# Three loads of 64 KiB rows put ahead of a decode-attention kernel's first load

## The chip, the cores and the metric

The kernel runs on one core of one Trainium2 chip. The time is device time in microseconds, from the start of the program to its end. The kernel before was timed in two runs: median 1936.92 us (1936.79 to 1937.05). A profile is one execution taken by the hardware profiler; its span goes from the first to the last instruction.

## What is computed

Two independent blocks, A and B, of the same shape. Each takes one new token for 2 batch rows, makes its query, attends over a cache of 8192 positions with 32 heads of 192, and projects the result. Everything is bf16.

```python
# x: (2, 1, 640)   k_cache, v_cache: (2, 32, 8192, 192)   wq: (640, 6144)   wo: (6144, 640)
def _A_ref(x, k_cache, v_cache, wq, wo):
    B, Sq, D = x.shape
    Hq, Dh = 32, 192
    Hkv = k_cache.shape[1]
    rep = Hq // Hkv                                   # 1
    q = (lambda x, *d: x.transpose(*d))((x @ wq).reshape(B, Sq, Hq, Dh), 0, 2, 1, 3)
    k = jnp.repeat(k_cache, rep, axis=1)
    v = jnp.repeat(v_cache, rep, axis=1)
    scores = jnp.einsum("bhqd,bhkd->bhqk", q, k) * (Dh ** -0.5)
    p = _softmax(scores, axis=-1)
    o = jnp.einsum("bhqk,bhkd->bhqd", p, v)
    return (lambda x, *d: x.transpose(*d))(o, 0, 2, 1, 3).reshape(B, Sq, Hq * Dh) @ wo
# B is the same with its own inputs; the two results are concatenated on the last axis
```

The four caches hold 2 x 32 x 8192 x 192 elements each, 805 MB in all, and each of their bytes is needed once. The four weights are 31 MB together.

## The kernel before

**Units.** The work on the caches is cut into 64 units (`NU`): 2 blocks, 16 pairs of heads, 2 batch rows. A unit loads one K tile and one V tile. Each tile is 128 rows of 49152 B: the first 64 rows are the 8192 positions of one head, 128 to a row, the other 64 those of the next head. A tile is 6144 KB.

**The large tile.** `big` has 86016 bf16 elements (172032 B) in each of its 128 partitions. Three buffers of 24576 elements (`kv[0]` to `kv[2]`) lie at its start, and the tiles take them in turn: K of unit 0, K of unit 1, V of unit 0, K of unit 2, V of unit 1 and so on (`loads`, line 213). Behind them are two areas of 6144 elements for the products. Before the first units run, the two query weights lie in the same bytes: A's from element 24576 on, B's from 55296 on (`wq_off`, line 186). At the end, the output weights lie there too.

**A unit.** VectorE multiplies a K tile with the query, broadcast over the positions, in four chunks (`dve_mul`, L290). TensorE sums the products over the 192 elements by matmuls with the identity (`pe_sum`, L367), VectorE finishes the sum and takes the maximum, GpSimd spreads the maximum over the partitions, ACT takes the exponentials, and TensorE makes the weighted sum of V (`pe_pv`, L381).

**The start.** The query of all heads is made first. The x rows are spread over the partitions by TensorE and VectorE (`pe_x`, L350, and `dve_xbc`, L276), then 32 products with the query weights (`pe_q`, L359) are copied out by VectorE and ACT (L280, L285). Nothing of it can begin before the two x rows have landed.

**SyncE's queue.** All loads but one go through SyncE, one after the other, in the order in which the code writes them out. `ld_first`, 4 KB from ACT's queue, is the exception; nothing reads what it loads, and only the output waits for it. Each engine's work is a list (`_Stream`), whose `add` takes a function that issues an instruction and the events to wait for; the wait stands on that engine, and what is behind it in the list waits too. The order on SyncE is: a first piece of A's query weight (4096 B of each of the 128 rows, 512 KB), the rest of it (57344 B of each, 7168 KB), x of A and of B, B's query weight (61440 B rows, 7680 KB), and then the tiles. A tile's load waits until the tile that held its buffer three loads earlier has been used. The first piece of the weight is issued before the block of the engine programs begins (line 493), all others inside.

`dma` (line 247) makes a load and gives it an event of its own; such an event has come when all of the load has landed.

Of the kernel before, what the change touches and what calls it, by code (L numbers as in the profile page):

```python
# [117 lines left out]
def build_kernel(nc, blocks, out):  # L118
# [28 lines left out]
    with ExitStack() as es:  # L147
# [7 lines left out]
        big = sb("big", [128, NBUF * BUFE + 2 * PRODE], BF16)  # L155
# [39 lines left out]
        S_sp = _Stream("sp", sem("s_sp"), reg)  # L195
# [6 lines left out]
        def dsem(k, n=1):  # L202
            reg[k] = (sem("d_" + "_".join(str(i) for i in k)), 16 * n)
# [4 lines left out]
        for blk in range(NBLK):  # L208
            dsem(("wq", blk), len(wq_cut[blk]))
            dsem(("odone", blk))  # L210
        dsem(("first",))

        loads = [("k", 0)]
        for u in range(1, NU):
# [13 lines left out]
        for blk, rows, off, w in ((0, (WR,), woA, [("s", LASTU, NCH - 1)]), (1, (29,), wo0, [("pv", LASTU - 1)]),  # L228
                                  (1, (11, 5, 2, 1), wo1, [("pv", LASTU)])):
            r = 29 if off == wo1 else 0  # L230
            for n in rows:
                pieces.append((blk, r, r + n, off, w))
                off, r, w = off + n * D, r + n, []
# [9 lines left out]
        def back(name, u, c, n):  # L243
            i = u * NCH + c - n
            return (name, i // NCH, i % NCH) if i >= 0 else None

        def dma(out_ap, in_ap, k):
            s = reg[k][0]
            return lambda eng: eng.dma_start(out_ap, in_ap).then_inc(s, 16)  # L249

        def ld_x(blk):
            return dma(x4[B * blk:B * blk + B, :], blocks[blk]["x"][:, 0, :], ("x",))

        def ld_wq(blk, n):
            lo, hi = wq_cut[blk][n]
            src = blocks[blk]["wq"].rearrange("(j c) n -> j (c n)", c=DC)
            return dma(big[:, wq_off[blk] + lo:wq_off[blk] + hi], src[:, lo:hi], ("wq", blk))

        def ld_wo(n):
            blk, r0, r1, off, _ = pieces[n]  # L260
            src = blocks[blk]["wo"].rearrange("(p i) n -> p (i n)", i=WR)
            return dma(big[:, off:off + (r1 - r0) * D], src[:, r0 * D:r1 * D], ("wo", n))
# [177 lines left out]
        for u in range(NU):  # L440
            for c in range(NCH):
                w = [("k", u), ("pq", NP - 1), ("qa", NP - 1), ("qx", NP - 1), back("s", u, c, 2)]
# [32 lines left out]
        for n, p in enumerate(pieces):  # L475
            w = [("wo", n), ("ot", p[0])]
# [8 lines left out]
        def done(i):  # L485
            if i < 0:
                return None
            kind, u = loads[i]
            return ("m", u, NCH - 1) if kind == "k" else ("pv", u)

        ld_first = dma(first[:], blocks[0]["wq"].rearrange("(j c) n -> j (c n)", c=DC)[0:128:8, 0:128], ("first",))
        ld_first(nc.scalar)
        ld_wq(0, 0)(nc.sync)
        S_sp.add(ld_wq(0, 1))
        for blk in range(NBLK):
            S_sp.add(ld_x(blk))
# [1 line left out]
        for i, (kind, u) in enumerate(loads):  # L498
            w = [done(i - NBUF)]
            if i in (1, 2):  # L500
                w = [("pq", PPB * i - 1)]
# [8 lines left out]
        for n in range(1, HP + 1):  # L510
            S_pool.add((lambda n: (lambda eng: eng.memset(tri[0:n, n:n + 1], 1.0)))(n),
                       waits=[("tri0",)] if n == 1 else [], sig=("tri",) if n == HP else None)
# [5 lines left out]
        for n in range(128 // HP):  # L518
# [3 lines left out]
                  waits=[("id1",), ("place0",)], sig=("place",))  # L522
# [50 lines left out]
def bass_concat_heads__gqa_block_cached__mha_block_cached__decode_kernel(  # L573
    nc: bass.Bass,
    A_x: bass.AP,
    A_k_cache: bass.AP,
    A_v_cache: bass.AP,
    A_wq: bass.AP,
    A_wo: bass.AP,
    B_x: bass.AP,  # L580
    B_k_cache: bass.AP,
    B_v_cache: bass.AP,
    B_wq: bass.AP,
    B_wo: bass.AP,
    out: bass.AP,
):
    blocks = [
        dict(x=A_x, k=A_k_cache, v=A_v_cache, wq=A_wq, wo=A_wo),
        dict(x=B_x, k=B_k_cache, v=B_v_cache, wq=B_wq, wo=B_wo),
    ]  # L590
    build_kernel(nc, blocks, out)
# [28 lines left out]
```

## Time and profile before

| what | value |
|---|---|
| median of two runs | 1936.92 us |
| the profiled execution: span | 1935.4 us |
| TensorE busy | 1507.4 us (78%) |
| VectorE busy | 1123.0 us (58%) |
| ACT, GpSimd busy | 142.4 us (7%), 28.6 us (1%) |
| read from DRAM | 836.77 MB |
| DMA time of SyncE's queue (q1), share of 16 engines | 99.9% |

The median is 1.5 us above the span of the profiled execution; of that execution the page gives the span and no other time. An engine's busy time counts its instructions, without waiting; the share of q1 counts the time that packets took on the 16 DMA engines. In the lists of groups, a line such as "L290 DVE" names the line of the kernel, the engine, what is written and read, the number of instructions, their busy time, the mean of one, and the idle time ahead of them with what ended it. "us to landing" in the lists of DMAs goes from the issue by the engine to the arrival of the last byte.

### The profile page before, as it was taken

To read this page: it belongs to the slowest core of one execution; us is meant where nothing else is said; L and a number is where in the kernel's file an instruction comes from. 1 tells how busy PE (TensorE), PEld (TensorE's weight loads), DVE (VectorE), ACT (ScalarE), POOL (GpSimd) and SP (SyncE) were. 2 spreads that over 40 slices of the span, in tenths; PEclk is the share of its full clock that TensorE was granted. 3 is DMA by queue.
4 is the path that set the end of the run, shared out by engine and by line. 5 is a ranking of instruction groups with operands and counts; after the bars stand their busy time and mean duration, and the time that the engine had idled before them with its cause. 6 is when DMAs were issued, how large, how long until landed. Compare 5 with 4: busy or idle time off the path is not lost.

```text
span 1935.4 us, 19062 instructions
## 1 busy us (share of the span) xinstructions
PE 1507.4 (78%) x7729; PEld 732.1 (38%) x7729; DVE 1123.0 (58%) x907; ACT 142.4 (7%) x519; POOL 28.6 (1%) x113
## 2 busy tenths in 40 slices
PE   5777878878878878878878877877877877877878
PEld 2333433433433433434433433433433433433434
DVE  4765565565565565565565565565565565565560
ACT  3100000000000000000000000000000000000000
POOL 0000000000000000000000000000000000000000
PEclk9899999999999999999999999999999999999998
DMA  9999999999999999999999999999999999999999
GB/s 423 424 435 438 430 434 437 434 431 437 436 429 436 437 430 434 438 432 433 437 436 428 437 435 430 436 437 430 435 437 432 433 437 435 430 436 437 429 435 394
DMA packets 19786, 836.92 MB, mean 432 GB/s; under 512 B 2232, under 2 KB 2368, under 8 KB 2752
## 3 DMA queue, kind: packets, MB, share of 16 engines
q1 hardware_dynamic: 19744, 836.78, 99.9%
q8 instruction: 6, 0.10, 0.0%
q14 instruction: 4, 0.03, 0.0%
q10 hardware_dynamic: 32, 0.00, 0.0%
HBM read 836.77 MB, written 0.01 MB: 432 GB/s over the span
## 4 chain that ended last, share of the span: by engine, by line
DMA 49%; PE 29%; DVE 17%; issue 5%; DVEq 0%; SPq 0%; ACT 0%; ACTq 0%
DMA big<-in_B_k_cache_dram 25%; DMA big<-in_A_k_cache_dram 22%; PE ops L381 18%; DVE big L290 15%; PE scps L367 9%; DVE sc L294 2%; DMA big<-in_B_wo_dram 1%; PE scps L359 1%; DMA xw<-in_B_x_dram 1%; PE outps L359 0%; PE ops L373 0%; DVEq L290 0%; DVE qall L280 0%; PE scps L409 0%; SPq L249 0%
## 5 line engine op out<-in xcount | busy, mean ns | idle before, releaser
L290 DVE TENSOR_TENSOR big<-big,qall 128x6144 bf16<-128x6144 bf16 x256 | 852.8, 3352 | 522.0 <-DMA big<-in_B_k_cache_dram 275.3
L367 PE MATMUL scps<-big,ident 128*128 128x512 bf16 x3072 | 777.8, 411 | 395.3 <-DVE big L290 393.0
L381 PE MATMUL ops<-big,pb 128*34 128x384 bf16 x4096 | 676.8, 326 | 0.0
L367 PEld LDWEIGHTS scps<-big,ident 128*128 128x128 bf16 x3072 | 303.3, 104 | 863.1 <-DVE big L290 483.6
L381 PEld LDWEIGHTS ops<-big,pb 128*34 128x34 bf16 x4096 | 395.5, 98 | 258.7
L294 DVE TENSOR_REDUCE sc<-scps 128x32 f32<-128x512 f32 x256 | 176.0, 687 | 196.8 <-PE scps L367 196.8
L320 ACT ACTIVATE nb<-mg 64x1 f32<-64x1 f32 x128 | 25.7, 201 | 1707.1 <-POOL mg L271 1706.4
L329 ACT ACTIVATE pb<-sc,nb 64x128 bf16<-64x128 f32 x128 | 55.8, 436 | 7.8
L271 POOL PARTITION_ALL_REDUCE mg<-mp x64 | 25.9, 404 | 1857.9 <-DVE mp L300 1857.9
L300 DVE TENSOR_REDUCE mp<-sc 64x1 f32<-64x128 f32 x128 | 35.9, 280 | 8.3
L314 ACT ACTIVATE qall<-o_sum,rc 2x192 f32 (+1 forms) x64 | 29.0, 453 | 20.7 <-DVE o_sum L311 19.1
L311 DVE TENSOR_TENSOR o_sum<-ops,o_hi 2x192 f32<-2x192 f32 x64 | 22.1, 345 | 7.7
L359 PE MATMUL scps<-big,xw 128*128 x120 | 23.2, 351 | 2.2 <-DVE xw L276 2.2
L329 ACT ACTIVATION_READ_ACCUMULATOR pb<-sc,nb 64x1 f32 x128 | 23.7, 185 | 0.0
L308 DVE COPY o_hi<-ops 2x192 f32<-2x192 f32 x64 | 22.3, 349 | 2.0
L305 DVE RECIPROCAL rc<-ops 2x1 f32<-2x1 f32 x64 | 10.0, 156 | 21.3 <-PE ops L381 19.3
L280 DVE CAST qall<-scps 64x192 f32 x48 | 17.0, 355 | 6.5 <-PE scps L359 4.5
L285 ACT ACTIVATE qall<-scps 64x192 f32 x48 | 15.6, 325 | 29.4 <-DVE qall L280 27.2
L350 PE MATMUL oTps<-ident,xw 4*128 4x4 bf16 x5 | 0.4, 178 | 21.5 <-DMA xw<-in_B_x_dram 21.5
L359 PEld LDWEIGHTS scps<-big,xw 128*128 128x128 bf16 x120 | 12.4, 103 | 11.4 <-issue 5.2
L373 PEld LDWEIGHTS ops<-ones,rs 128*2 128x2 f32 x128 | 5.5, 82 | 26.9 <-issue 26.9
L409 PE MATMUL outps<-big,oT 128*2 128x320 bf16 x96 | 9.5, 375 | 5.5 <-DMA big<-in_A_wo_dram 5.5
(36 smaller groups left out, 67.9 us busy)
## 6 DMA issues: line engine op xcount, KB each, us to landing
big<-in_A_k_cache_dram SPq DMA_DIRECT2D x32, 6144.0 KB, 28.9
big<-in_A_v_cache_dram SPq DMA_DIRECT2D x32, 6144.0 KB, 27.9
big<-in_B_k_cache_dram SPq DMA_DIRECT2D x32, 6144.0 KB, 28.9
big<-in_B_v_cache_dram SPq DMA_DIRECT2D x32, 6144.0 KB, 27.9
big<-in_B_wq_dram SPq DMA_DIRECT2D x1, 7680.0 KB, 37.1
big<-in_A_wo_dram SPq DMA_DIRECT2D x1, 7680.0 KB, 30.0
big<-in_A_wq_dram SPq DMA_DIRECT2D x1, 7168.0 KB, 20.2
big<-in_B_wo_dram SPq DMA_DIRECT2D x1, 4640.0 KB, 30.3
```

The costliest lines, as they stand in the source:

```text
L271: return lambda eng: eng.partition_all_reduce(mg[u % 3][:], mp[u % 3][:], 128, bass.bass_isa.ReduceOp.max)
L290: return lambda eng: eng.tensor_tensor(prod[c % 2], t[:, c * TC:(c + 1) * TC, :], qall[:, S_dve.at(u), :].broadcast_to([128, TC, Dh]), ALU ...
L294: return lambda eng: eng.tensor_reduce(sc[u % 3][:, c * TC:(c + 1) * TC], scps[(u * NCH + c) % 3][:], AXL.X, ALU.add)
L300: ins = eng.tensor_reduce(mp[u % 3][r, s:s + 1], sc[u % 3][r, :], AXL.X, ALU.max)
L308: return lambda eng: eng.tensor_copy(o_hi[:], ops[u % 3][32:34, Dh:QW])
L311: return lambda eng: eng.tensor_tensor(o_sum[:], ops[u % 3][0:2, 0:Dh], o_hi[:], ALU.add)
L314: return lambda eng: eng.activation(qall[0:2, S_act.at(u), :], o_sum[:].unsqueeze(1), ACTF.Identity, scale=rc[u % 3][:])
L320: ins = eng.activation(nb[u % 3][r, :], mg[u % 3][r, s:s + 1], ACTF.Identity, scale=-scale)
L329: ins = eng.activation(dst, sc[u % 3][r, :].rearrange("p (g j a) -> p g a j", j=JB, a=2), ACTF.Exp, bias=nb[u % 3][r, :], scale=scale, acc ...
L359: ins = eng.matmul(qps[hp % NQ][:, 0:QW], xbc[:, blk, c, :], wq_t[blk][:, c, S_pe.at(off, QW, QW)], start=(c == 0), stop=(c == DC - 1))
L367: ins = eng.matmul(scps[(u * NCH + c) % 3][:], ident[:], prod[c % 2][:, :, j * DG:(j + 1) * DG], start=(j == 0), stop=(j == NJ - 1))
L381: ins = eng.matmul(ops[u % 3][0:MP, 0:QW], pb[u % 3][:, j0s:j0s + MP], vv[:, j, :], start=(j == 0), stop=(j == TJ - 1))
```

## The change

Three loads are put ahead of everything else on SyncE's queue. Their source is the A block's K cache, taken as 128 rows of 196608 B (8 heads of batch row 0 laid end to end). Load n takes bytes 65536 n to 65536 n + 65535 of each row, 32768 elements, 8192 KB in all 128 rows. In each partition of `big` the first lands on elements 0 to 32767, the second on 32960 to 65727, the third on 256 to 33023. The third overlaps both of the others, so it waits until these have landed. The first piece of A's query weight, which lands on elements from 24576 on, now waits for the third, and is issued inside the block like the rest. Nothing reads what the three loads bring; the weights and the tiles are loaded over it.

```diff
@@ -209,6 +209,8 @@
             dsem(("wq", blk), len(wq_cut[blk]))
             dsem(("odone", blk))
         dsem(("first",))
+        for n in range(3):
+            dsem(("row", n))
 
         loads = [("k", 0)]
         for u in range(1, NU):
@@ -247,6 +249,10 @@
         def dma(out_ap, in_ap, k):
             s = reg[k][0]
             return lambda eng: eng.dma_start(out_ap, in_ap).then_inc(s, 16)
+
+        def ld_row(n, off):
+            src = blocks[0]["k"][0, 0:8].rearrange("h t d -> (h t d)").rearrange("(p n) -> p n", p=128)
+            return dma(big[:, off:off + 32768], src[:, n * 32768:(n + 1) * 32768], ("row", n))
 
         def ld_x(blk):
             return dma(x4[B * blk:B * blk + B, :], blocks[blk]["x"][:, 0, :], ("x",))
@@ -490,7 +496,9 @@
 
         ld_first = dma(first[:], blocks[0]["wq"].rearrange("(j c) n -> j (c n)", c=DC)[0:128:8, 0:128], ("first",))
         ld_first(nc.scalar)
-        ld_wq(0, 0)(nc.sync)
+        for n, (off, w) in enumerate(((0, []), (32768 + 192, []), (256, [("row", 0), ("row", 1)]))):
+            S_sp.add(ld_row(n, off), waits=w)
+        S_sp.add(ld_wq(0, 0), waits=[("row", 2)])
         S_sp.add(ld_wq(0, 1))
         for blk in range(NBLK):
             S_sp.add(ld_x(blk))
```

At the start of SyncE's program there stood before (a name as `s_pe` is the event count of an engine, the branch leads into the block of the engine programs):

```order
L249 DMA big<-in_A_wq_dram 128x2048 [waits barrier_Pool_Activation_PE_DVE_SP_release]
L549 UNCONDITIONAL_BRANCH
L249 DMA big<-in_A_wq_dram 128x28672
L249 DMA xw<-in_A_x_dram 2x640
L249 DMA xw<-in_B_x_dram 2x640
L249 DMA big<-in_B_wq_dram 128x30720
L249 DMA big<-in_A_k_cache_dram 128x24576
L249 DMA big<-in_A_k_cache_dram 128x24576 [waits s_pe]
```

And there stands now (`d_row_0` to `d_row_2` are the events of the three loads):

```order
L557 UNCONDITIONAL_BRANCH [waits barrier_Pool_Activation_PE_DVE_SP_release]
L251 DMA big<-in_A_k_cache_dram 128x32768 x2
L251 DMA big<-in_A_k_cache_dram 128x32768 [waits d_row_1,d_row_0]
L251 DMA big<-in_A_wq_dram 128x2048 [waits d_row_2]
L251 DMA big<-in_A_wq_dram 128x28672
L251 DMA xw<-in_A_x_dram 2x640
L251 DMA xw<-in_B_x_dram 2x640
L251 DMA big<-in_B_wq_dram 128x30720
L251 DMA big<-in_A_k_cache_dram 128x24576
L251 DMA big<-in_A_k_cache_dram 128x24576 [waits s_pe]
```

The first piece of the weight has moved from ahead of the branch to behind it and behind the three new loads, with a wait of its own; from there on the order is the same. The other engines have the same instructions in the same order.

## The prediction

> **What bounds the kernel now.** I read the page first: the row of slices, the queues and the costliest groups of instructions.
>
> ```profile
> span 1935.4 us, 19062 instructions
> PE 1507.4 (78%) x7729; PEld 732.1 (38%) x7729; DVE 1123.0 (58%) x907; ACT 142.4 (7%) x519; POOL 28.6 (1%) x113
> DMA  9999999999999999999999999999999999999999
> q1 hardware_dynamic: 19744, 836.78, 99.9%
> HBM read 836.77 MB, written 0.01 MB: 432 GB/s over the span
> L290 DVE TENSOR_TENSOR big<-big,qall 128x6144 bf16<-128x6144 bf16 x256 | 852.8, 3352 | 522.0 <-DMA big<-in_B_k_cache_dram 275.3
> ```
>
> Of the 16 DMA engines' time, 99.9% is spent on packets of one queue, q1, SyncE's. It moves 836.78 MB. No other engine comes near its span: TensorE has 78%, VectorE 58%. The last line says what VectorE's products wait for: 522.0 us of idle time before them, most of it ended by a transfer that landed. The table of waits has the same thing by block:
>
> ```profile
> DVE big L290 <- DMA big<-in_B_k_cache_dram: 275.3, 32, 9.3
> DVE big L290 <- DMA big<-in_A_k_cache_dram: 245.7, 30, 9.8
> ```
>
> The product is late for its K tile in 62 of 64 units. The table by windows then says whether there is any stretch in which the queue rests, so that an added transfer could go there. Columns: busy us of PE, PEld, DVE, ACT, POOL with counts, granted clock, DMA share, GB/s.
>
> ```profile
> 0.00:10.00 10.00, 0.00 (x0) 0.00 (x0) 1.12 (x5) 1.69 (x3) 2.71 (x49) 1.00 0.82 328
> 10.00:20.00 10.00, 0.00 (x0) 0.00 (x0) 0.00 (x0) 0.00 (x0) 0.00 (x0) 1.00 1.06 459
> 20.00:40.00 20.00, 16.27 (x86) 9.15 (x87) 12.18 (x34) 8.97 (x28) 0.00 (x0) 1.00 1.00 433
> 40.00:60.00 20.00, 14.66 (x85) 8.24 (x84) 17.12 (x37) 11.85 (x37) 0.00 (x0) 0.93 1.00 433
> 60.00:80.00 20.00, 15.27 (x55) 5.80 (x54) 17.77 (x11) 0.00 (x0) 3.06 (x1) 0.84 1.00 431
> 80.00:110.00 30.00, 26.15 (x134) 12.36 (x133) 21.15 (x15) 2.80 (x12) 0.72 (x2) 0.98 1.02 443
> 110.00:140.00 30.00, 22.88 (x112) 10.88 (x110) 16.13 (x12) 1.85 (x7) 0.36 (x1) 0.89 0.98 423
> 140.00:1890.00 1750.00, 1375.72 (x6896) 665.20 (x6897) 1034.85 (x790) 112.95 (x427) 21.73 (x61) 0.95 1.00 434
> 1920.00:1935.40 15.40, 13.44 (x166) 7.16 (x162) 0.96 (x2) 0.85 (x2) 0.00 (x0) 0.97 0.75 314
> ```
>
> Bytes are booked where a packet stands in the record, so a short window can read 459 GB/s beside one that reads 328; the first 20 us together are 394. From 20 us on the rate is 423 to 443 in each stretch, and over the 1750 us of the loop it is 434 GB/s at a share of 1.00. The queue rests only in the last 15 us (0.75), when every load has been issued and the output goes out, and while it starts. So this kernel is one stream of bytes, and the end comes when the stream has passed.
>
> **The change, part by part.** The three added loads are each 128 x 65536 B = 8.389 MB, together 25.166 MB. They go through the same SyncE queue ahead of everything else, and the first useful load now waits for the last of them.
>
> *The bytes.* 25.166 MB is to the byte four tiles of K or V (6144 KB each, four times is 24576 KB, three times 8192 KB as well). At the loop's 434 GB/s it takes 25.166 / 0.434 = 58.0 us. The trace holds the same quantity as a time. In the steady loop a unit loads one K and one V tile, so two units are this many bytes, and the chain of waits shows three starts of the K transfer, two units each apart:
>
> ```profile
> 157.63 28.18 DMA big<-in_A_k_cache_dram
> ...
> 215.59 28.18 DMA big<-in_A_k_cache_dram
> ...
> 273.09 28.69 DMA big<-in_A_k_cache_dram
> ```
>
> 215.59 - 157.63 = 57.96 and 273.09 - 215.59 = 57.50. I take 58.0. For the bounds I take the best and the worst 30 us stretch of the table above: 443 GB/s gives 56.8 us, 423 gives 59.5.
>
> The Trainium skill, in HBM Reference, "Specifications (TRN2)", gives about 358 GB/s as the effective rate of one core; by that the three loads would take 70.3 us and the sum below would come to 2012. The loop's 434 GB/s over 1750 us speaks against it here: the rate of this lone core is the one in the trace.
>
> Do longer rows change the rate? The trace has no row of 65536 B. Its nearest are the 61440 B rows of the second query weight (7680 KB in 128 rows), against the 49152 B rows of K and V (6144 KB in 128 rows):
>
> ```profile
> big<-in_B_wq_dram SPq DMA_DIRECT2D x1, 7680.0 KB, 37.1
> big<-in_A_wq_dram SPq DMA_DIRECT2D x1, 7168.0 KB, 20.2
> big<-in_A_wq_dram SPq DMA_DIRECT2D x1, 512.0 KB, 3.7
> first<-in_A_wq_dram ACTq DMA_DIRECT2D x1, 4.0 KB, 2.9
> ...
> 0.72 0.87 SPq L249 DMA_DIRECT2D big<-in_A_wq_dram  x2
> ...
> 2.30 0.36 SPq L249 DMA_DIRECT2D big<-in_B_wq_dram  x1
> 2.70 37.74 SPq L249 DMA_DIRECT2D big<-in_A_k_cache_dram  x2
> ...
> 2.01 19.49 DMA xw<-in_B_x_dram
> ```
>
> These are four rows of the DMA issues (the last number is us from issue to landing), three of SyncE's timeline and one of the chain. The second weight is issued at 2.30 and lands 37.1 us later, at 39.4. The small x load just ahead of it on the queue lands at 2.01 + 19.49 = 21.5. Between the two lie 7.864 MB in 17.9 us: 439 GB/s. Rows of 61440 B run no slower than those of 49152 B, and I price those of 65536 B alike.
>
> *The two waits.* The third load writes over parts of both others and waits for them; the first piece of the query weight waits for the third. At each wait the queue is empty and stays so until the landing has been seen, the next load is issued and its first bytes arrive. The loop has no such stop, so I bound it by loads that met an empty queue. The 512 KB piece, first on SyncE's queue, took 3.7 us from issue to landing, of which its own 0.524 MB take 1.2 at the loop's rate: 2.5 over. The 4 KB load on ACT's queue, with next to no bytes, took 2.9. The whole opening, from the issue at 0.72 to x's landing at 21.5, is 20.8 us for 7.869 MB, which take 18.1: 2.7 over. I take 2.5, since that row is the same queue at the same place, with all 128 partitions. Ends: 0, if issue and landing hid entirely under bytes that still move (which an empty queue rules out, so it is only a floor), and 3.7, the whole of that row. Seeing the landing costs SyncE little: the chain has 0.02 us of "issue" between a PE end and the next issue.
>
> ```profile
> 157.61 0.02 issue
> ```
>
> How many times is 2.5 paid? Loads one and two go out back to back, without a wait: one start and one landing for 38.7 us of bytes. Load three: one more start and landing for 19.3 us. The weight's own start, after the second wait, was paid before the change too. So twice: 5.0 us, and 0.04 for the two reactions of SyncE.
>
> *The place in the program.* Before, the weight's first piece stood ahead of the block's entry branch; now all SyncE loads stand behind it. The pair of weight issues with the branch between took 0.87 us; the two issues alone are the row below (398 to 420 ns each, 0.82 in all), so the branch is worth 0.05 us.
>
> ```profile
> L249 SPq DMA_DIRECT2D big<-in_A_wq_dram x2: 398/409/420, 0.7 to 1.2; - x2
> ```
>
> The issues of loads two and three, at 0.33 to 0.42 us: the second lies under the first's bytes, the third is inside the 2.5.
>
> *Who waits behind this.* Everything on SyncE's queue: both weights, both x rows, then all 128 tiles, in the same order with the same waits. TensorE's first step stands and waits for x (a row of the table of waits; the two below it are the timeline's last rows of preparation):
>
> ```profile
> PE oTps L350 <- DMA xw<-in_B_x_dram: 21.5, 1, 21.5
> ...
> 2.80 0.46 DVE L521 COPY place<-ident 2x2 bf16<-2x2 bf16 x1
> ...
> 2.94 0.30 POOL L517 MEMSET pb<- 128x256 bf16 x1
> ```
>
> It now waits some 63 us longer, and with it the whole chain of query products. The fills on GpSimd and the identity's copies on VectorE end at 2.94 + 0.30 = 3.2 and 2.80 + 0.46 = 3.3 us, long before x: they hid under the stream and gain nothing. No engine can do anything of use while the three loads run, since every datum comes later on the same queue. Nothing is removed, and the loop and the tail keep their relative times.
>
> *Sum.* 58.0 + 5.0 + 0.04 + 0.05 = 63.1 us. On the profiled execution's span: 1935.4 + 63.1 = 1998.5. The median of the two timed runs is 1936.92, 1.5 us above that span, an offset that I carry over: 1936.9 + 63.1 = **2000.0 us**, 3.3% above before.
>
> **The rivals.** A difference of 2% is 38.7 us here, about what a measurement of this kernel can tell from no change: within 1898.2 and 1975.7.
>
> *The added loads run slower than the stream (9%).* Their rows are 196608 B apart, 3 times 65536, so at any moment all the rows that are read together have the same address modulo 65536, and in DRAM they could meet in the same place and be served in turn. K and V rows are 49152 B apart, so only every fourth one agrees in this way; the weight rows are 61440 B apart. If pairs of rows took turns, the three loads would run at 217 GB/s: 116 us, and 116 + 5.1 = 121 on top, 2058 us. Against it: in K's tiles every fourth row is exactly 196608 B from the next, so streams with this distance already run at 434 GB/s in the loop. The Trainium skill, in DMA: Bandwidth & Descriptors, "Latency and other measured facts", lists copies whose row pitch is a large power of two: 512 KiB still near the full rate, 4 MiB at half. The pitch here is no power of two and is smaller than any of those, and no run here shows such a pitch; the rule leaves this case open rather than predicts it. I hold it for the least unlikely surprise.
>
> *The loads do not move their bytes (3%), the other side.* 65536 is above every row length in the trace (61440 at most). If a row of this length counted as empty somewhere between the instruction and the engines, nothing downstream would notice, as nothing reads these bytes; the semaphores would still arrive. Then only the two stops stand: 2 x 2.5 + 0.1 = 5.1, 1942.0 us, and the kernel is not slower by the 2%. It decides as soon as one of three loads' bytes takes under about 10 us instead of 19.3 in all three. Against it: each length in the trace up to 61440 B is priced by its bytes.
>
> *Part of the delay is won back (7%).* The loop might catch up where the queue rests. But it rests for 0.1% of 1935.4 us, 1.9 us; even if all of that were recovered, the time would be 2000.0 - 1.9 = 1998.1. The case where the loop has slack against its transfers would need VectorE to find its tiles ready, and the waits above say it finds them late 62 times.
>
> **How the numbers follow.** The forecast as summed has 81%, the slow loads 9%, the won-back part 7%, the empty loads 3%. The forecast's own ends: at best 56.8 with stops of 0, 1993.7; at worst 59.5 with two stops of 3.7 and 0.1, 67.0, which is 2003.9. One thing is added above: a wait pays for the last of 16 engines, and if that engine is a whole row behind, 65536 B at a sixteenth of 434 GB/s are another 2.4 us: 2006.3. So 1994 to 2007, which takes in the won-back case and leaves out the slow and the empty loads, 12% together. Slower by over 2% is the forecast, the won-back part and the slow loads, 97%, of which I give a point away for what I have not thought of: 96%. Within 2% is the case of empty loads, 3%. Faster by over 2% has no mechanism: 1%.
>
> **What would show it.** In the profile after: HBM bytes read 25.17 MB more (836.77 to 861.94); SyncE's first two issues near 0.8 us, the third near 42 (0.8 + 38.7 + 2.5), the weight's first near 64; x landing near 84.6 instead of 21.5; from there every time of before plus 63. The second and third of the three loads carry the price of a byte: two loads back to back land about 41.2 us after the first issue, the third 21.8 after its own. If the third takes 41 instead, the address pattern is the cause; if it takes 3, the bytes were not moved; if it takes 21.8 but the third's issue comes more than 1 us after the second's landing, the stop was mis-sized. The prediction is wrong if the shift at x is not the shift at the end.

## The result and the profile after

The changed kernel takes 2000.11 us (two runs, 2000.11 to 2000.12) against 1936.92 before: ratio 1.0326, 95% interval 1.0296 to 1.0356. It is slower by 63.2 us; 63.1 had been forecast. The span of the profiled execution is 1998.6 us.

The head of the page after the change, with the lines that answer to those of before:

```profile
span 1998.6 us, 19065 instructions
PE 1507.9 (75%) x7728; PEld 731.0 (37%) x7729; DVE 1122.2 (56%) x907; ACT 142.4 (7%) x519; POOL 28.5 (1%) x113
q1 hardware_dynamic: 20176, 861.95, 99.7%
HBM read 861.94 MB, written 0.01 MB: 431 GB/s over the span
L296 DVE TENSOR_TENSOR big<-big,qall 128x6144 bf16<-128x6144 bf16 x256 | 852.8, 3352 | 518.1 <-DMA big<-in_B_k_cache_dram 261.9
```

TensorE, VectorE, ACT and GpSimd have the same busy time as before, to 1.1 us. What is more are the bytes: 861.94 - 836.77 = 25.17 MB, all of the three loads. The queue's share went from 99.9 to 99.7%; it now stands empty twice. Where that is, the table by windows shows (busy us of PE, PEld, DVE, ACT, POOL with counts, granted clock, DMA share, GB/s):

```profile
43.00:43.50 0.50, 0.00 (x0) 0.00 (x0) 0.00 (x0) 0.00 (x0) 0.00 (x0) 1.00 5.97 1966
45.00:62.00 17.00, 0.00 (x0) 0.00 (x0) 0.00 (x0) 0.00 (x0) 0.00 (x0) 1.00 1.00 432
60.50:61.25 0.75, 0.00 (x0) 0.00 (x0) 0.00 (x0) 0.00 (x0) 0.00 (x0) 1.00 3.23 1398
61.25:64.75 3.50, 0.00 (x0) 0.00 (x0) 0.00 (x0) 0.00 (x0) 0.00 (x0) 1.00 0.00 0
140.00:1950.00 1810.00, 1424.22 (x7115) 686.01 (x7116) 1072.96 (x811) 115.83 (x439) 25.39 (x63) 0.95 1.00 434
```

The third load runs at 432 GB/s with no other engine at work, and the loop moves 434 GB/s as before.

The short windows must be read with care: a packet, here one row of 65536 B, is booked whole, bytes and time, in the window in which it starts. The first row above shows it. It books 15 packets of 3.2 us each within half a microsecond, less than 1.5 us after the third load's issue at 42.06. So the zero from 61.25 to 64.75 us says that no packet starts there, not that nothing moves: the 16 packets that start from 60.50 to 61.25 take 2.4 us each. The trace's list of packets, with the start of each and the time that it took, gives the gaps themselves. The last packet of the third load ends at 63.64 us, and the first one of the weight starts at 64.96; between the second and the third load nothing is under way from 41.62 to 43.01. In the kernel before, the list has no such gap before the tail.

The steps one by one stand in the chain of waits and in SyncE's timeline:

```profile
1.18 40.80 DMA big<-in_A_k_cache_dram
42.06 21.91 DMA big<-in_A_k_cache_dram
...
65.21 19.90 DMA xw<-in_B_x_dram
```

```profile
63.99 0.81 SPq L251 DMA_DIRECT2D big<-in_A_wq_dram  x2
...
116.97 0.33 SPq L251 DMA_DIRECT2D big<-in_A_v_cache_dram  x1
...
1931.32 0.33 SPq L251 DMA_DIRECT2D big<-in_B_v_cache_dram  x1
```

The second of the two loads that go together lands at 1.18 + 40.80 = 41.98 us; the third is issued at 42.06 and lands 21.91 later; the weight follows at 63.99, 63.3 us after its 0.72 of before. x lands at 85.11, where it landed at 21.5 before. The first V tile is issued 63.7 us later than before, the last one 63.2 later; before, they stood here:

```profile
53.24 0.33 SPq L249 DMA_DIRECT2D big<-in_A_v_cache_dram  x1
...
1868.09 0.33 SPq L249 DMA_DIRECT2D big<-in_B_v_cache_dram  x1
```

### The profile page after: what moved, and what is told of

The parts are those of the page before. It is cut to its first block, busy times and chain, and to the rows that moved or that the text cites. A ratio compares the mean times of both kernels' runs of the same rounds, so it can differ in the third digit from the quotient of the medians.

```text
span 1998.6 us, 19065 instructions
## 1 busy us (share of the span) xinstructions
PE 1507.9 (75%) x7728; PEld 731.0 (37%) x7729; DVE 1122.2 (56%) x907; ACT 142.4 (7%) x519; POOL 28.5 (1%) x113
## 3 DMA queue, kind: packets, MB, share of 16 engines
q1 hardware_dynamic: 20176, 861.95, 99.7%
HBM read 861.94 MB, written 0.01 MB: 431 GB/s over the span
## 4 chain that ended last, share of the span: by engine, by line
DMA 51%; PE 26%; DVE 17%; issue 6%; DVEq 0%; SPq 0%; ACT 0%; ACTq 0%
DMA big<-in_A_k_cache_dram 25%; DMA big<-in_B_k_cache_dram 23%; PE ops L387 17%; DVE big L296 15%; PE scps L373 7%; DVE sc L300 2%; DMA big<-in_B_wo_dram 1%; PE scps L365 1%; DMA xw<-in_B_x_dram 1%; PE outps L365 0%; PE ops L379 0%; DVEq L296 0%; DVE qall L286 0%; SPq L251 0%; PE scps L415 0%
## 5 line engine op out<-in xcount | busy, mean ns | idle before, releaser
L365 PEld LDWEIGHTS scps<-big,xw 128*128 128x128 bf16 x120 | 12.4, 103 | 11.4 <-issue 5.2
```

The lines of the kernel that those rows point to most:

```text
L365: ins = eng.matmul(qps[hp % NQ][:, 0:QW], xbc[:, blk, c, :], wq_t[blk][:, c, S_pe.at(off, QW, QW)], start=(c == 0), stop=(c == DC - 1))
```

## Experiments

Two theories for the 63 us were set against each other. Theory A is the prediction's: 58.0 us of bytes at the stream's rate, and a stop of about 2.5 us for each time the queue runs empty. Theory B has the same total in another way: no price for stops, and bytes of these rows at 399 GB/s. A third question was the rival that didn't occur here, rows whose addresses agree. The kernel before, timed on the same chip beside each group of runs, took 1936.99 and 1937.01 us.

**The waits without the bytes.** Only 512 B of each row are loaded; the rest of the three loads is left out.

```diff
-            return dma(big[:, off:off + 32768], src[:, n * 32768:(n + 1) * 32768], ("row", n))
+            return dma(big[:, off:off + 256], src[:, n * 32768:n * 32768 + 256], ("row", n))
```

> Both waits and all three loads stay, but each load brings only the first 512 B of each row (0.197 MB in all, 0.5 us at the loop's 434 GB/s). Theory A (the added time is 58.0 us of bytes and two stops of 2.5 us): 1936.9 + 0.5 + 5.1 = 1942.5. Theory B (stops cost nothing; the rows of 64 KiB run at 399 GB/s instead of 434, 25.17 MB in 63.1 us): 1937.4.

Measured: 1941.45 us (1941.16 to 1941.75), ratio 1.0023 (1.0014 to 1.0032), 4.5 us more than before. Theory B, with 0.5, is out. Theory A's 5.6 is 1.1 too much. The chain and SyncE's timeline show where. The execution that they show is one of the longest of this run, 1941.73 us, and issues the weight 4.81 us later than before:

```profile
1.18 2.39 DMA big<-in_A_k_cache_dram
3.65 1.87 DMA big<-in_A_k_cache_dram
```

```profile
0.72 3.25 SPq L251 DMA_DIRECT2D big<-in_A_k_cache_dram  x3
5.53 0.81 SPq L251 DMA_DIRECT2D big<-in_A_wq_dram  x2
```

The first two loads, from the issue at 0.72 to the landing at 3.57, take 2.55 us over their 0.30 us of bytes, about as much as allowed; 0.46 of that is the second issue, which has few bytes to hide under here. The third load, 66 KB, takes 1.87 us from issue to landing, 1.72 over its bytes where 2.5 had been allowed: most of the miss. This is the smallest stop that these runs show: issue, way there, landing, with nearly no bytes.

**Half the bytes.** Rows of 32768 B; the second half of each load is left out.

```diff
-            return dma(big[:, off:off + 32768], src[:, n * 32768:(n + 1) * 32768], ("row", n))
+            return dma(big[:, off:off + 16384], src[:, n * 32768:n * 32768 + 16384], ("row", n))
```

> The three loads bring only the first 32768 B of each of their rows, half the bytes (12.58 MB), with the same distance between rows and the same waits. Theory A (bytes at 434 GB/s and two stops of 2.5): 29.0 + 5.1, 1971.0. If a stop's price grew with the row (its first packets are slow in proportion to their length), the stops would come to about 2.2 each: 1970.4.

Measured: 1970.66 us (1970.49 to 1970.81), ratio 1.0174 (1.0159 to 1.019). That is 33.65 us more than before; less 29.0 of bytes, 4.65 for two stops, 2.3 each. The time lies between the two forecasts, 0.3 us from either, and doesn't decide between them. The traces do. The third load of this run, beside that of the kernel after, which took 21.91:

```profile
22.56 12.03 DMA big<-in_A_k_cache_dram
```

12.03 less its 9.66 us of bytes (4.194 MB) is 2.4; 21.91 less 19.33 is 2.6; with 512 B rows it was 1.87 less 0.15. So the time over the bytes goes up from 1.7 to 2.4 to 2.6 with the row. The lists of packets show what grows. After an empty queue the first 16 packets of the third load are slow: 3.14 us on average, where the later ones take 2.42, in the kernel after; 1.64 for 1.21 here; 0.03 for 0.03 with 512 B rows. The other parts hardly change between the three: 1.0 us from the issue to the first packet, 0.3 from the end of the last packet to the landing, and 0.4 to 0.7 because the packets do not all start and end together. Later packets cost the same by the byte at every length: 2.42 us for 65536 B, 1.21 for 32768 B, 1.82 for the 49152 B of K and V.

**One stop fewer.** The third load goes to the bytes of the first, so that it needs to wait for the first only, and is issued while the second still moves.

```diff
-        for n, (off, w) in enumerate(((0, []), (32768 + 192, []), (256, [("row", 0), ("row", 1)]))):
+        for n, (off, w) in enumerate(((0, []), (32768 + 192, []), (0, [("row", 0)]))):
             S_sp.add(ld_row(n, off), waits=w)
-        S_sp.add(ld_wq(0, 0), waits=[("row", 2)])
+        S_sp.add(ld_wq(0, 0), waits=[("row", 1), ("row", 2)])
```

> All bytes as changed. The third load lands on the bytes of the first alone and waits for it alone, so it is issued while the second still moves; the queue empties once instead of twice. The weight waits for the second and the third. Theory A: 2000.1 - 2.5 = 1997.6. Theory B: 2000.1.

Measured: 1997.61 us (1997.37 to 1997.84), ratio 1.0312 (1.0298 to 1.0327). The forecast of theory A was 1997.6; against the kernel after, 2.5 us are gone with the bytes unchanged. In the chain, the first load lands at 0.72 + 21.93 = 22.65 us, while the second is under way, and the third is issued and lands 38.58 us later:

```profile
0.72 21.93 DMA big<-in_A_k_cache_dram
22.67 38.58 DMA big<-in_A_k_cache_dram
```

From landing to landing these are the 38.7 us of two loads' bytes, with no time over them: the third's start is covered by the second.

**One stop more.** The second load waits for the first as well.

```diff
-        for n, (off, w) in enumerate(((0, []), (32768 + 192, []), (256, [("row", 0), ("row", 1)]))):
+        for n, (off, w) in enumerate(((0, []), (32768 + 192, [("row", 0)]), (256, [("row", 0), ("row", 1)]))):
```

> All bytes as changed. The second load, too, waits for the first, so the queue empties three times instead of twice. Theory A: 2000.1 + 2.5 = 2002.6. Theory B: 2000.1.

Measured: 2002.33 us (2002.15 to 2003.08), ratio 1.0338 (1.0324 to 1.0352), 2.2 more than the kernel after. The three loads now stand alone in the chain:

```profile
0.72 21.92 DMA big<-in_A_k_cache_dram
22.66 21.76 DMA big<-in_A_k_cache_dram
44.44 21.72 DMA big<-in_A_k_cache_dram
```

Each takes 21.7 to 21.9 us, 19.3 of bytes and 2.4 to 2.6 over. With one, two and three stops the time is 1997.61, 2000.11 and 2002.33: the bytes are the same in all three, so the stops are what differs, and theory B falls again. The lists of packets agree: ahead of the weight there are one, two and three gaps of 1.3 to 1.4 us in which no packet of the queue is under way.

**All waits, no stop.** The loads are laid so that each wait ends while another load moves. Rows are 61440 B here, so that they fit the place of B's weight; the last 4096 B of each are left out.

```diff
-            return dma(big[:, off:off + 32768], src[:, n * 32768:(n + 1) * 32768], ("row", n))
+            return dma(big[:, off:off + 30720], src[:, n * 32768:n * 32768 + 30720], ("row", n))
...
-        for n, (off, w) in enumerate(((0, []), (32768 + 192, []), (256, [("row", 0), ("row", 1)]))):
+        for n, (off, w) in enumerate(((BUFE + WQE, []), (0, []), (BUFE + WQE, [("row", 0)]))):
             S_sp.add(ld_row(n, off), waits=w)
-        S_sp.add(ld_wq(0, 0), waits=[("row", 2)])
+        S_sp.add(ld_wq(0, 0), waits=[("row", 1)])
...
-        S_sp.add(ld_wq(1, 0))
+        S_sp.add(ld_wq(1, 0), waits=[("row", 2)])
```

> Three loads of rows of 61440 B (23.59 MB), laid so that each wait is met while another load is still moving: the first and the third land where B's weight goes, the second where A's weight goes; the third waits for the first, A's weight for the second, B's weight for the third. All waits stay, but the queue is not empty at any of them. Theory A: 54.4 us of bytes and no stop, 1991.3; with two stops it would be 1996.4. Theory C (a wait costs by itself, whether the queue is empty or not): 1996.4.

Measured: 1991.31 us (1991.09 to 1991.61), ratio 1.0281 (1.0267 to 1.0295): 54.3 us more than before, for 54.4 us of bytes. The table of SyncE's waits says that it still waited three times:

```profile
SPq L251 <- DMA big<-in_A_k_cache_dram: 54.2, 3, 19.8
```

The list of packets has no gap here before the tail. So a wait of 18 us on average costs nothing when the queue has bytes behind it, and theory C, with 1996.4, is out. What is paid for is the empty queue, not the wait.

**Rows 1 MiB apart.** Same bytes, same places in the large tile, same waits; only the source differs.

```diff
-            src = blocks[0]["k"][0, 0:8].rearrange("h t d -> (h t d)").rearrange("(p n) -> p n", p=128)
+            src = blocks[0]["k"].rearrange("b h t d -> (b h t d)")[0:128 * 524288].rearrange("(p n) -> p n", p=128)
```

> The three loads keep their bytes, their places in the large tile and their waits, but their rows are 1048576 B apart in DRAM instead of 196608. Theory A, with a rate that does not hang on the address: 2000.1. The rival of the prediction (rows whose addresses agree take turns), which was not seen at 196608: if pairs take turns here, 116 us of bytes and 2058. In between, the ratio that the Trainium skill, DMA: Bandwidth & Descriptors, Latency and other measured facts, gives for a pitch of 2 MiB against 512 KiB (164 against 207 GB/s) would make 73 us of the 58, and 2015.

Measured: 2011.48 us (2010.73 to 2012.08), ratio 1.0383 (1.0367 to 1.0399), 11.4 us above the kernel after. None of the three forecasts holds, though 2015 is near: the rate does hang on where the rows lie, but the 58 us more that pairs taking turns would cost aren't there. The chain shows both parts of the loads longer, 48.74 for 40.80 and 25.86 for 21.91:

```profile
1.18 48.74 DMA big<-in_A_k_cache_dram
50.00 25.86 DMA big<-in_A_k_cache_dram
```

If the 11.4 us are put to the 58.0 us of bytes, these run at 25.17 / 69.4 = 363 GB/s. The table by windows agrees for the first two loads, with the DMA engines busy all the time:

```profile
2.00:48.00 46.00, 0.00 (x0) 0.00 (x0) 1.12 (x5) 0.86 (x3) 1.24 (x12) 1.00 1.00 365
```

Two runs ask what it is in the distance.

**Rows 1 MiB and 4 KiB apart.** `524288` becomes `526336` elements in the line above.

> As the run with rows 1048576 B apart, which took 2011.5, but with 1052672 B from row to row (4096 more). If the loss of 11 us there came from rows whose addresses agree in their low 20 bits, it is gone: 2000.1. If it came from the rows lying far apart in DRAM (134 MB in all instead of 25), it stays: 2011.5. The Trainium skill, DMA: Bandwidth & Descriptors, Latency and other measured facts, reports that 4 KiB of padding brought the full rate back at a larger pitch.

Measured: 2000.21 us (2000.13 to 2001.42), ratio 1.0329 (1.0313 to 1.0345). The loss is gone, and the loads take what they take in the kernel after:

```profile
1.18 40.95 DMA big<-in_A_k_cache_dram
42.20 21.90 DMA big<-in_A_k_cache_dram
```

**Rows 512 KiB apart.** `524288` becomes `262144`.

> Rows 524288 B apart. If the loss hangs on the agreement of low address bits, it is between the one at 196608 (none) and the one at 1048576 (11.4 us): 2000 to 2011. If only the distance counted, in proportion (67 MB in all against 134 and 25): about 2004.

Measured: 2000.81 us (2000.61 to 2001.07), ratio 1.033 (1.0314 to 1.0346): 0.7 above the kernel after. The loads of the profiled execution take 0.4 and 0.3 longer than there:

```profile
1.18 41.19 DMA big<-in_A_k_cache_dram
42.45 22.19 DMA big<-in_A_k_cache_dram
```

That is little beside 11.4. Distance by itself doesn't count, then: the padded rows spread over as much of DRAM as those of 1 MiB and run at the full rate. It is the agreement of addresses, and nearly all of the loss sets in between 512 KiB and 1 MiB. The Trainium skill, in DMA: Bandwidth & Descriptors, "Latency and other measured facts", has this for copies within DRAM (near the full rate at 512 KiB, less at 2 MiB, restored at 4 MiB by 4 KiB of padding). The loads here go the same way, with nearly the full rate at 512 KiB, 363 GB/s at 1 MiB and the full rate with the padding. What in the DRAM makes the rows meet isn't shown.

## Why the prediction was right

- *The queue bounds.* Shown. 25.17 MB more took the time of 25.17 MB; with half of the bytes, half; and no other engine's busy time changed by more than 1.1 us.
- *58.0 us of bytes.* Held: in the run with one stop fewer, two loads took 38.58 us from landing to landing, for 38.7. The four tiles with the same number of bytes in the loop (57.96 us between two K issues) were the right row to price them by. Rows of 65536 B are no dearer than those of 61440 or 49152.
- *Two stops of 2.5 us.* Right in sum: 63.2 - 58.0 - 0.1 = 5.1. One stop taken away saved 2.5, one added cost 2.2. That 2.5 fitted so well is in part luck. The price hangs on the row, from 1.7 us for 512 B to 2.6 for 65536 B, mostly because the first packets after an empty queue are slow; the prediction took it from a load with rows of 4096 B, and allowed for long rows only at the upper end of its range. With 512 B rows the two stops came to 4.5 with their bytes, where 5.6 had been expected.
- *0.05 us for the place behind the branch.* Not shown. The first issue stands at 0.72 us in both traces. The 0.05 was the time between two issues: after the change the two pieces of the weight are 0.05 apart as well (64.32 to 64.37 in the chain), with no branch between them.
- *The shift stays to the end.* Yes, within 0.5 us. At the weight's first issue it is 63.3, at x 85.1 - 21.5 = 63.6, at the first V tile 63.7, at the last V tile and in the span 63.2. The opening behind the weight's issue took 21.1 us for 20.8, which is within what this stretch varies: it took 20.6 in the run with half the bytes and 20.8 in the one with one stop fewer. The whole delay is there when the weight is issued, and the loop neither adds to it nor takes from it. The prediction's 84.6 for x is 0.5 early.
- *The rivals.* The slow loads didn't come at this distance, but a loss that hangs on the agreement of the rows' addresses exists on this chip, at 1 MiB, with a sixth of the rate lost rather than half; whether rows take turns there isn't shown. The empty loads are out: the page counts the bytes as read. Nothing was won back: the shift is 63.3 us at the weight's issue and 63.2 at the end.
- *The rate by the Trainium skill.* The sentence that priced the bytes at 358 GB/s by HBM Reference of the Trainium skill took only half of what its section says: the same section gives a core that streams alone about 425 GB/s. The loop's 434 is near that figure, 2% above it.

## What to carry to other kernels

Where the queue's share is 1.00 or close to it in every window between the start and the tail, an added load costs its bytes at the rate of the loop, and the best price is a stretch of the same trace that moves as many bytes. A wait between two loads costs only if nothing else stands in the queue behind the load that is waited for; then it was 1.7 to 2.6 us here, more with longer rows, and laying the loads so that another one moves at that time takes it to nothing. Source rows that lie 1 MiB apart were worth 4 KiB of padding, which saved 11 us of 69; at 512 KiB there was less than 1 us to save.

## What the runs showed that was not expected

The 4 KB load on ACT's queue, issued at 0.7 us in both kernels, took 2.9 us to land before, and 7.4 after:

```profile
first<-in_A_wq_dram ACTq DMA_DIRECT2D x1, 4.0 KB, 7.4
```

After the change its bytes meet a queue of 64 KiB rows, where before there were rows of 4096 B. It cost nothing, since only the output waits for it, but a small load that is needed early would have been 4.5 us late. The traces of the other runs have the same load beside other rows: 2.0 us beside rows of 512 B, 4.8 beside 32768 B, 7.1 beside 61440 B, 7.4 to 7.8 beside 65536 B, and 9.3 in the run at 1 MiB, whose packets took longer. So it goes with the time that the rows beside it take. No run was made for this, and what holds the small load up isn't shown.
